# Turning q of two batches with TensorE transposes, weight sums on GpSimd, one halo copy a batch

## The chip, the cores and the metric

The kernel runs on one core of one Trainium2 chip. The metric is device time in microseconds (us) of one execution. All data are fp32; the engines are TensorE (PE), VectorE (DVE), ScalarE (ACT), GpSimd (POOL) and SyncE (SP, which here only issues DMAs).

## The reference

A linear attention without softmax, an RMS norm, and a gated linear unit whose gate is a causal convolution over five tokens:

```python
# q, k, v: (8 batches, 8 heads, 576 tokens, 64); w_val, w_out: (512, 512); conv_w: (5, 512)
kv  = einsum('bhsd,bhse->bhde', k, v)
o   = einsum('bhsd,bhde->bhse', q, kv)
x   = o / sqrt(mean(o * o, -1) + 1e-6) * g_norm        # heads side by side: (8, 576, 512)
gate_pre[t] = sum(conv_w[i] * x[t - 4 + i] for i in range(5))
out = (sigmoid(gate_pre) * (x @ w_val)) @ w_out
```

## The kernel before

The work is cut into small steps, each a Python function with a batch and a piece as arguments (`turn_q_rows 0 3` turns block 3 of batch 0). A long string `PLAN` (lines 19 to 204) lists the steps, and they are emitted in that order, so each engine's queue is the plan's order cut down to that engine's instructions. A tile framework adds the semaphore waits: an instruction waits for whoever wrote what it reads, read what it overwrites, or held its buffer before. PSUM is used as eight banks that are handed on from tile to tile.

**q.** The tokens of a batch are stored as 32 runs (t) of 18 (n), so that a token's neighbours lie 32 columns apart. For batches 0 and 1, `load_q_rows` puts q into the tile `qs` with the partition as (head, t) for four heads, once for each half r of the heads, and 18 rows n of 64 values in the free direction. `turn_q_rows b j` (line 471) turns a block j of four rows n (two in block 4) into a PSUM tile: for each n and r one matmul against the identity puts the 64 values of that half of the heads onto 64 partitions. `sort_q b j` (line 481) copies the tile to `qT`, 128 partitions at once, and sorts heads before tokens. Later batches are turned by DVE (`turn_q`).

**From q to the value product.** `kv_product` multiplies k and v, `kv_copy` (L450 for batch 0, L453 for others) takes the result out of PSUM, `raw_whole` (L512, batch 0) and `raw_pair` (L501) multiply qT with it; `square` (ACT), `sums` (DVE) and `powers` (POOL, L552) make the inverse root, `normalise` makes x, `turn_x` (PE, L583) and `keep_x` (ACT, L590) or, from batch 2 on, `turn_blocks` (DVE, L596) and `move_blocks` (DMA from SP and POOL, L604) make `xT`: channels on partitions, tokens in the free direction, with 128 columns ahead of them for the halo.

**The halo.** The first tokens of a run need the last four of the run before. `halo b` (line 608) fills the 128 columns in front from the last ones, shifted by one run, with one GpSimd copy (L611) for each of the four channel blocks kc. `gate_start` (ACT, L615), four `gate_tap` (DVE, L621) and `gate_end` (ACT, L628) make the gate.

**The weights.** They come as float64 and are narrowed on the chip in eight steps each (`narrow_weight`, L363 to L389 on DVE, L368 to L372 on ACT); this runs beside batches 0 and 1. The convolution weights (`cw`) come first: their steps on DVE and ACT end in `turn_cw` (PE, L414) and `keep_cw` (DVE, L418 to L420).

**The products.** Batches 0 and 1 use a plain value product (`val_product`, L633). From batch 2 on, and for the output product of all batches, the kernel uses a scheme with seven half-size products instead of eight (`val_fast`, L682, and `fast_product`, L774). It needs sums of blocks of the weights: `val_sums n` (line 649, into `vsum`) and `weight_sums n` (line 732, into `wsum`), four of each, 128 partitions x 512 elements, once for the whole kernel, on DVE. `x_sums` and `token_sums` make the sums of the other side.

Around the steps that matter most the plan reads (cut):

```
turn_q_rows 0 3; turn_q_rows 0 2; turn_q_rows 0 0; kv_product 0 0; turn_q_rows 0 1; sort_q 0 0; sort_q 0 1;
narrow_weight cw 0 3; narrow_weight cw 0 4; narrow_weight cw 0 7; turn_q_rows 0 4; turn_cw; keep_cw;
kv_product 0 1; sort_q 0 4; sort_q 0 3; kv_copy 0 0; kv_copy 0 1; ...; sort_q 0 2; raw_whole 0 3
...
move_blocks 2 0; move_blocks 2 2; move_blocks 2 1; ...; weight_sums 3; ...; kv_product 3 1; ...;
fast_product 0 0 6; move_blocks 2 3; raw_pair 3 3
```

Of the kernel before, what the change touches and what calls it, by code (L numbers as in the profile page):

```python
# [12 lines left out]
ALU = mybir.AluOpType  # L13
AX = mybir.AxisListType

P = 128
# [191 lines left out]
def kernel(  # L208
# [11 lines left out]
    nc = tc.nc  # L220
    B, H, S, D = q.shape
# [5 lines left out]
    NK = C // P  # L227
    TB = 32
    NB = S // TB
    K = moe_conv_w.shape[0]  # L230
    HALO = (K - 1) * TB
    SX = HALO + S
    HB = P // TB
# [19 lines left out]
    def ps(shape, name):  # L253
        return psum.tile(shape, FP32, tag="bank", bufs=8, name=name)
# [3 lines left out]
    ident = const.tile([P, P], FP32, name="ident")  # L258
    mhalf = const.tile([P, NJ * H + H // 2], FP32, name="mhalf")
    xTs = [const.tile([P, NK, SX], FP32, name=f"xT{i}") for i in range(2)]  # L260
# [9 lines left out]
    vsum = const.tile([P, 4, NK // 2, C // 2], FP32, name="vsum")  # L270
    wsum = const.tile([P, 4, NK // 2, C // 2], FP32, name="wsum")
    ys = [const.tile([P, C // TB, NJ, TB], FP32, name=f"y{i}") for i in range(2)]
    qs = const.tile([P, 3, NB, D], FP32, name="qs")
# [22 lines left out]
    st = {}  # L296
# [158 lines left out]
    def new_qT(b):  # L455
        if ("qT", b) not in st:
            st["qT", b] = work.tile([P, HP, S], FP32, tag="qT", name=f"qT{b}")
        return st["qT", b]
# [12 lines left out]
    def turn_q_rows(b, j):  # L471

        m = min(HB, NB - j * HB)
        pq = ps([P, HB, P], f"qTps{b}_{j}")
        for n in range(m):
            for r in range(2):
                nc.tensor.matmul(  # L477
                    pq[r * D:(r + 1) * D, n, :], qs[:, r, j * HB + n, :], ident[:], start=True, stop=True)
        st["pq", b, j] = pq

    def sort_q(b, j):

        m = min(HB, NB - j * HB)
        nc.scalar.copy(
            out=new_qT(b)[:].rearrange("p h (n t) -> p n h t", t=TB)[:, j * HB:j * HB + m],
            in_=st["pq", b, j][:, 0:m].rearrange("p n (h t) -> p n h t", t=TB))

    def raw_product(b, *chunks):

# [116 lines left out]
                in_=y[a * TB:(a + 1) * TB, i])  # L606

    def halo(b):
        for kc in range(NK):
            row = xTs[b % 2][:, kc, :].rearrange("p (n t) -> p n t", t=TB)  # L610
            nc.gpsimd.tensor_copy(row[:, 0:K - 1, 1:TB], row[:, NB:NB + K - 1, 0:TB - 1])  # L611

    def gate_start(b, jt):
        gate = work.tile([P, S], FP32, tag="gate", bufs=GATES, name=f"gate{b}_{jt}")
# [34 lines left out]
    def val_sums(n):  # L649

        one, two, op = (
            (wval[:, EVEN, HIGH], wval[:, ODD, HIGH], ALU.add),
            (vsum[:, 0], wval[:, EVEN, LOW], ALU.subtract),
            (wval[:, EVEN, LOW], wval[:, EVEN, HIGH], ALU.subtract),
            (wval[:, ODD, LOW], vsum[:, 1], ALU.subtract))[n]
        nc.vector.tensor_tensor(out=vsum[:, n], in0=one, in1=two, op=op)

    def x_sums(b, n):

# [72 lines left out]
    def weight_sums(n):  # L732
        one, two = (
            (wout[:, EVEN, HIGH], wout[:, EVEN, LOW]), (wout[:, ODD, HIGH], wsum[:, 0]),
            (wout[:, ODD, HIGH], wout[:, EVEN, HIGH]), (wout[:, ODD, LOW], wsum[:, 1]))[n]
        nc.vector.tensor_tensor(out=wsum[:, n], in0=one, in1=two, op=ALU.subtract)

    def token_sums(i, h, n):

# [62 lines left out]
    def store(i, c, queue=nc.sync, blocks=range(HB)):  # L802
# [5 lines left out]
    steps = {f.__name__: f for f in (  # L808
        load_half, load_q, load_q_rows, stage_weight, narrow_weight, turn_cw, keep_cw, start_warm, warm_up,
        kv_product, kv_copy, turn_q, turn_q_rows, sort_q, raw_whole, raw_pair, raw_tail, square, sums, powers, normalise,  # L810
        turn_x, keep_x, turn_blocks, move_blocks, halo, gate_start, gate_tap, gate_end, val_product, keep_val, gated,
        val_sums, x_sums, val_fast, val_keep, out_product, keep_out, weight_sums, token_sums, fast_product, fast_keep,
        store, store_last)}
    with tc.manual_schedule():
# [34 lines left out]
```

## Time and profile before

| | |
|---|---|
| timed runs | 305.83 and 306.24 us, median 306.03 |
| profiled execution, first to last instruction (span) | 304.6 us |
| the profiled execution's own time | not listed apart; the timed runs lie 1.2 to 1.6 us above the span |
| mean granted TensorE clock | 0.993 |
| PE busy | 294.8 us, 97% of the span |
| DVE busy | 269.2 us, 88% |
| ACT busy | 193.7 us, 64% |
| POOL busy | 114.9 us, 38% |
| PE on the turn (L477) | 144 records, 11.0 us |
| ACT on sort_q (L484) | 10 copies, 583 ns (512 columns) or 346 ns (256) each |
| DVE on the weight sums (L656, L736) | 8 instructions, 641 to 768 ns each |
| POOL on the halo (L611) | 32 copies, 17.5 us |

The profile is of one execution. A line of the groups names source line, engine, operation, tiles and shape, then busy time, mean duration and the idle time before. In the timeline a line gives start and duration in us, engine, line and operation; the square bracket says how long the engine had been idle and what released it. An fp32 matmul is two records, a transpose one. A queue's name with q (SPq) stands for the engine that issues a DMA. Matmul ends are modelled, so a busy PE can still be a PE that waits for little things.

### The profile page before, as it was taken

To read this page: it belongs to the slowest core of one execution; us is meant where nothing else is said; L and a number is where in the kernel's file an instruction comes from. 1 tells how busy PE (TensorE), PEld (TensorE's weight loads), DVE (VectorE), ACT (ScalarE), POOL (GpSimd) and SP (SyncE) were. 2 spreads that over 40 slices of the span, in tenths; PEclk is the share of its full clock that TensorE was granted. 3 is DMA by queue.
4 is the path that set the end of the run, shared out by engine and by line. 5 is a ranking of instruction groups with operands and counts; after the bars stand their busy time and mean duration, and the time that the engine had idled before them with its cause. 6 is when DMAs were issued, how large, how long until landed. Compare 5 with 4: busy or idle time off the path is not lost.

```text
span 304.6 us, 8977 instructions
## 1 busy us (share of the span) xinstructions
PE 294.8 (97%) x3441; PEld 232.4 (76%) x3441; DVE 269.2 (88%) x474; ACT 193.7 (64%) x596; POOL 114.9 (38%) x127
## 2 busy tenths in 40 slices
PE   7899999999999999999999999999999999999993
PEld 7788778877787785777778757787878588888582
DVE  1169999999999999999999999999999999999612
ACT  1569989999768664884586547683787354535220
POOL 3027354406568217364338352345536631000000
PEclk9979999999999999999999999999999999999999
DMA  7999998088569756988689477927411621112423
GB/s 269 343 368 343 272 302 210 4 230 269 154 147 329 231 163 167 269 220 260 173 253 294 111 175 232 326 72 214 114 48 30 169 80 34 36 42 64 103 69 103
DMA packets 32074, 55.53 MB, mean 182 GB/s; under 512 B 6166, under 2 KB 14358, under 8 KB 32032
## 3 DMA queue, kind: packets, MB, share of 16 engines
q1 hardware_dynamic: 29520, 49.76, 55.7%
q0 software_dynamic: 1632, 3.17, 4.1%
q10 hardware_dynamic: 880, 2.03, 1.8%
q8 instruction: 27, 0.44, 0.6%
q14 instruction: 15, 0.12, 0.1%
HBM read 39.21 MB, written 9.44 MB: 160 GB/s over the span
## 4 chain that ended last, share of the span: by engine, by line
PE 89%; DVE 5%; DMA 2%; issue 1%; ACT 1%; DVEq 0%; ACTq 0%; SPq 0%
PE a L774 18%; PE cb L774 14%; PE va L682 13%; PE val L633 11%; PE vc L682 6%; PE kvps L440 6%; PE raw L501 5%; PE out L720 5%; PE vb L682 4%; PE qTps L477 4%; PE raw L512 2%; PE xTps L583 2%; DMA qs<-in_q_dram 2%; DVE gate L621 2%; DVE xs L667 1%
## 5 line engine op out<-in xcount | busy, mean ns | idle before, releaser
L552 POOL TENSOR_TENSOR rt<-ss,mhalf 128x8 f32<-128x8 f32 (+3 forms) x38 | 68.9, 1822 | 101.0 <-DVE ss L544 100.8
L621 DVE SCALAR_TENSOR_TENSOR gate<-xT,cwT,gate 128x576 f32<-128x576 f32 x128 | 101.8, 809 | 1.0
L571 ACT ACTIVATE x<-raw,rt 128x64 f32<-128x64 f32 x252 | 55.8, 351 | 7.2 <-POOL rt L552 4.2
L604 POOL DMA_DIRECT2D xT<-y x48 | 26.4, 557 | 25.5 <-DVE ot L784 14.0
L633 PE MATMUL val<-xT,wval 128*128 128x288 f32 x128 | 33.0, 411 | 0.0
L774 PE MATMUL a<-wsum,sums 128*128 128x256 f32 x128 | 32.4, 382 | 0.0
L628 ACT ACTIVATE gate<-gate 128x576 f32<-128x576 f32 x32 | 22.0, 692 | 11.7 <-DVE gate L621 11.4
L633 PEld LDWEIGHTS val<-xT,wval 128*128 128x128 f32 x128 | 23.5, 190 | 6.5 <-ACT xT L590 0.4
L544 DVE TENSOR_REDUCE ss<-sq 128x8 f32<-128x520 f32 (+1 forms) x40 | 24.7, 627 | 2.9 <-ACT sq L531 2.5
L774 PEld LDWEIGHTS a<-wsum,sums 128*128 128x128 f32 x128 | 24.0, 190 | 4.1 <-issue 0.6
L535 ACT ACTIVATE sq<-raw 128x256 f32<-128x256 f32 (+1 forms) x70 | 22.4, 403 | 7.3 <-PE raw L501 7.1
L682 PE MATMUL va<-xs,vsum 128*128 128x288 f32 x96 | 26.6, 409 | 0.0
L615 ACT ACTIVATE gate<-xT,cwT 128x576 f32<-128x576 f32 x32 | 25.2, 811 | 1.5 <-DVE gv L646 1.3
L646 DVE TENSOR_TENSOR gv<-gv,gate 128x576 f32<-128x576 f32 x32 | 23.6, 750 | 0.9 <-ACT gate L628 0.8
L682 PEld LDWEIGHTS va<-xs,vsum 128*128 128x128 f32 x96 | 18.0, 190 | 5.1 <-ACT x L571 0.4
L611 POOL COPY xT<-xT 128x124 f32<-128x124 f32 x32 | 17.5, 585 | 10.5 <-ACT xT L590 10.5
L501 PEld LDWEIGHTS raw<-kv,qT 64*64 64x64 f32 x1008 | 16.4, 134 | 5.3 <-issue 3.0
L440 PEld LDWEIGHTS kvps<-v,k 64*64 64x64 f32 x1008 | 15.9, 135 | 3.7 <-issue 1.9
L501 PE MATMUL raw<-kv,qT 64*64 64x64 f32 x1008 | 18.7, 221 | 0.0
L440 PE MATMUL kvps<-v,k 64*64 64x64 f32 x1008 | 17.6, 220 | 0.0
L774 PE MATMUL cb<-wsum,sums 128*128 128x256 f32 x64 | 16.9, 386 | 0.1
L774 PE MATMUL cb<-wout,gv 128*128 128x256 f32 x64 | 16.8, 385 | 0.0
(111 smaller groups left out, 542.3 us busy)
## 6 DMA issues: line engine op xcount, KB each, us to landing
qs<-in_q_dram SPq DMA_DIRECT2D x96, 140.0 KB, 4.2
out_dram<-ot SPq DMA_DIRECT2D x140, 64.0 KB, 1.7
k<-in_k_dram SPq DMA_DIRECT2D x14, 576.0 KB, 6.3
v<-in_v_dram SPq DMA_DIRECT2D x12, 576.0 KB, 6.5
xT<-y SPq DMA_DIRECT2D x48, 64.0 KB, 2.7
xT<-y POOLq DMA_DIRECT2D x48, 64.0 KB, 3.3
y<-in_moe_w_val_dram SPq DMA_DIRECT2D x4, 512.0 KB, 11.4
w_wout<-in_moe_w_out_dram SPq DMA_DIRECT2D x4, 512.0 KB, 6.3
```

The lines of the kernel that those rows point to most:

```text
L440: nc.tensor.matmul(st["kvps", b][s][r * D:(r + 1) * D, i], st["k", b, i][rows, r, cols], st["v", b, i][rows, r, cols], start=(j == 0), sto ...
L501: nc.tensor.matmul(st["raw", b, c][r][cols, to * D:(to + 1) * D], st["qT", b][rows, hp, first:first + D], kvs[b % 2][rows, hp, :], start=T ...
L544: nc.vector.reduce_sum(out=st["ss", b][:, FIRST[c]:FIRST[c] + n], in_=st["sq", b, c][:, 0:n], axis=AX.X)
L552: nc.gpsimd.tensor_tensor(out=st["rt", b][:, which], in0=st["ss", b][:, which], in1=mhalf[:, which], op=ALU.pow)
L571: nc.scalar.activation(out=x[:, to * D:(to + 1) * D], in_=raw[:, h * D:(h + 1) * D], func=AF.Copy, scale=root[:, to:to + 1])
L604: (nc.sync if i % 2 else nc.gpsimd).dma_start(out=xTs[b % 2][i * TB:(i + 1) * TB, :, first:first + P], in_=y[a * TB:(a + 1) * TB, i])
L615: nc.scalar.activation(out=gate[:], in_=xTs[b % 2][:, jt, HALO:SX], func=AF.Copy, scale=cwT[:, K - 1, jt:jt + 1])
L621: nc.vector.scalar_tensor_tensor(out=gate[:], in0=xTs[b % 2][:, jt, tap * TB:tap * TB + S], scalar=cwT[:, tap, jt:jt + 1], in1=gate[:], op ...
L633: nc.tensor.matmul(val[:], wval[:, kc, jt * P:(jt + 1) * P], xTs[b % 2][:, kc, HALO + n * SV:HALO + (n + 1) * SV], start=(kc == 0), stop=( ...
L646: nc.vector.tensor_tensor(out=both, in0=both, in1=st["gate", b, jt][:], op=ALU.mult)
L682: nc.tensor.matmul(st[bank, "val", b, mj][:], weights_[:, k], tokens()[:, k], start=(n in (0, 1, 3) and k == 0), stop=(k == NK // 2 - 1), ...
L774: nc.tensor.matmul(st[bank, i, p], tokens()[:, k], weights_[:, k], start=(n < 2 and k == 0), stop=(k == NK // 2 - 1), skip_group_check=True)
```

## The change

Four edits; the plan stays as it is.

1. `turn_q_rows` transposes two rows n and n+1 at once (128 partitions x 128 values), so half e of the result's partitions holds the row of parity e. Half as many PE instructions are issued, each over the full width, and as transposes.
2. `sort_q` now makes four copies a block, one for each half r of the heads and parity e, from 64 partitions of PSUM to 64 of `qT`; where e is not r, they shift the data by 64 partitions. In batch 0 the two copies with e = 1 are on DVE, all others are on ACT.
3. `val_sums` and `weight_sums` run on GpSimd, at the same places in the plan.
4. `halo` is one GpSimd copy of all four channel blocks.

```diff
     def turn_q_rows(b, j):
         m = min(HB, NB - j * HB)
-        pq = ps([P, HB, P], f"qTps{b}_{j}")
-        for n in range(m):
-            for r in range(2):
-                nc.tensor.matmul(
-                    pq[r * D:(r + 1) * D, n, :], qs[:, r, j * HB + n, :], ident[:], start=True, stop=True)
+        pq = ps([P, 2, HB // 2, P], f"qTps{b}_{j}")
+        for r in range(2):
+            for n in range(0, m, 2):
+                nc.tensor.transpose(
+                    pq[:, r, n // 2, :], qs[:, r, j * HB + n:j * HB + n + 2, :].rearrange("p n d -> p (n d)"),
+                    ident[:])
         st["pq", b, j] = pq

     def sort_q(b, j):
         m = min(HB, NB - j * HB)
-        nc.scalar.copy(
-            out=new_qT(b)[:].rearrange("p h (n t) -> p n h t", t=TB)[:, j * HB:j * HB + m],
-            in_=st["pq", b, j][:, 0:m].rearrange("p n (h t) -> p n h t", t=TB))
+        for r in range(2):
+            for e in range(2):
+                (nc.vector.tensor_copy if b == 0 and e else nc.scalar.copy)(
+                    out=new_qT(b)[r * D:(r + 1) * D].rearrange("p h (n t) -> p n h t", t=TB)[
+                        :, j * HB + e:j * HB + m:2],
+                    in_=st["pq", b, j][e * D:(e + 1) * D, r, 0:m // 2].rearrange("p n (h t) -> p n h t", t=TB))
...
     def halo(b):
-        for kc in range(NK):
-            row = xTs[b % 2][:, kc, :].rearrange("p (n t) -> p n t", t=TB)
-            nc.gpsimd.tensor_copy(row[:, 0:K - 1, 1:TB], row[:, NB:NB + K - 1, 0:TB - 1])
+        rows = xTs[b % 2][:].rearrange("p k (n t) -> p k n t", t=TB)
+        nc.gpsimd.tensor_copy(rows[:, :, 0:K - 1, 1:TB], rows[:, :, NB:NB + K - 1, 0:TB - 1])
...
     def val_sums(n):
-        nc.vector.tensor_tensor(out=vsum[:, n], in0=one, in1=two, op=op)
+        nc.gpsimd.tensor_tensor(out=vsum[:, n], in0=one, in1=two, op=op)
...
     def weight_sums(n):
-        nc.vector.tensor_tensor(out=wsum[:, n], in0=one, in1=two, op=ALU.subtract)
+        nc.gpsimd.tensor_tensor(out=wsum[:, n], in0=one, in1=two, op=ALU.subtract)
```

## The prediction

> **What bounds the kernel now.** I read the busy shares, then the chain that ended last, then stretches of 5 us, then the timeline at the places the change touches.
>
> ```profile
> PE 294.8 (97%) x3441; PEld 232.4 (76%) x3441; DVE 269.2 (88%) x474; ACT 193.7 (64%) x596; POOL 114.9 (38%) x127
> ...
> PE 89%; DVE 5%; DMA 2%; issue 1%; ACT 1%; DVEq 0%; ACTq 0%; SPq 0%
> ```
>
> The chain lies on TensorE: time leaves the kernel only if PE work goes or PE's waits shrink, and a wait put on PE is not won back, since PE hardly idles later. But an average hides the stages:
>
> ```profile
> 15.00:20.00 5.00, 4.39 (x89) 3.82 (x89) 3.18 (x9) 3.38 (x9) 0.00 (x0) 0.73 0.95 341
> ...
> 25.00:30.00 5.00, 5.00 (x122) 4.32 (x122) 4.73 (x10) 4.57 (x9) 4.03 (x2) 1.00 0.86 321
> 30.00:35.00 5.00, 5.00 (x112) 4.06 (x104) 4.93 (x9) 4.68 (x11) 2.45 (x4) 1.00 0.95 293
> ...
> 45.00:50.00 5.00, 5.00 (x85) 3.93 (x84) 5.00 (x9) 5.00 (x21) 2.46 (x3) 1.00 1.05 254
> ```
>
> The columns after the stretch are its sum, then PE, PEld, DVE, ACT and POOL busy. From 25 to 80 us ACT is as full as PE (4.57, 4.68, 5.00 of 5), though its share of the span is 64%; the edited copies stand exactly there. DVE too is full from 30 us to 280 us.
>
> ```profile
> 6.12 5.05 PE L477 MATMUL qTps<-ident,qs 128*64 128x128 f32 x48 [0.70 <-DMA qs<-in_q_dram]
> ...
> 16.56 1.09 ACT L450 COPY kvbd<-kvps 64x128 f32<-64x128 f32 x4 [1.51 <-PE kvps L440]
> 17.15 6.32 PE L512 MATMUL raw<-kvbd,qT 128*128 128x128 f32 x40 [0.56 <-ACT kvbd L450]
> ...
> 23.40 2.84 PE L477 MATMUL qTps<-ident,qs 128*64 128x128 f32 x48
> ...
> 25.43 1.07 ACT L484 COPY qT<-qTps 128x512 f32<-128x512 f32 x2
> ...
> 29.97 2.04 ACT L590 ACTIVATE xT<-xTps 128x512 f32<-128x512 f32 x4
> ...
> 31.16 2.11 PE L633 MATMUL val<-xT,wval 128*128 128x288 f32 x8
> ```
>
> The releasers show who leads: kv_copy (L450) frees the raw products; keep_x (L590) frees the first val_product, 0.33 us after the copy it needs.
>
> **Part 1, the turn on PE.** Each block of four rows was 8 matmuls (16 records), now 4 transposes. The rows: 48 records in 2.77 us at 23.4 us (58 ns each, chain) against, for a transpose of 128x128:
>
> ```profile
> L583 PE MATMUL xTps<-ident,x 128*128 128x128 f32 x48 | 7.6, 281 | 0.0
> ```
>
> These start 109 ns apart. Batch 1 (18 rows): 4.23 us become 18 x 0.109 = 1.96, 2.3 us less. Batch 0 saves more, its first 48 records taking 5.05 us at half pace. Both are covered. Batch 0: the kv product that follows can start when k and v land (9.5 us instead of 11.1), but the second one stands behind turn_cw at 15.05, which waits for the conv-weight step on ACT (13.93); that one waits for no turn. Batch 1: what follows waits for ACT (next part). The earlier turns also free qs sooner for SP's loads of batch 1's q (issued at 13.88), and all behind them on SP; the DMA share is 0.94 and 0.95 of 10 to 20 us, so they land hardly earlier. I count nothing for PE; without the cover it would be 2.3 us, less in batch 0.
>
> **Part 2, the copies of batch 0.** One ACT copy a block (0.58 us) becomes four of 64 partitions, two on ACT, two on DVE. In the order of the built instructions each waits for the one before: ACT's second waits for DVE's first. Nearest rows: ACT 128x256 in 0.35 us (L484's short block), DVE 128x256 from PSUM in 0.42 (L797); of short blocks ACT 0.26 (L450), DVE about 0.29. Blocks 0 and 1 run 11.4 to 14.3 us, while ACT and DVE were idle, and leave L372 at about 13.9. Blocks 4 and 3 are caught: their DVE copies stand behind keep_cw, which ends at 15.92. From there 0.29 (DVE) + 0.26 (ACT) + 0.29 (DVE) + 0.42 (DVE) + 0.35 (ACT), with a little for the hand-overs, gives kv_copy at 17.5 instead of 16.56: +0.95. Block 2 then takes 0.35 + 0.42 + 0.35 instead of 0.58: +0.55. ACT is 1.5 us late; of that it gives back 0.99 in its wait for PE at 21.72. **+0.55** enters batch 1.
>
> The clock adds to it. The turns at 6.12 run at 105 ns a record, at 12.31 at 61; the clock rose at 10.5 after a stretch full of matmuls, and the 15 to 20 stretch, with gaps in it, was granted 0.73. After the change PE is idle from 8.7 to 9.5 and from about 12 to 15, so it may stay slow until 24 us: 24 raw records at 213 ns instead of 112 for part of the way, +0.9 on ACT's wait for the last raw product. Bounds 0 and 0.9; I take half, **+0.45**.
>
> The Trainium skill (TensorE: Matmul & The Clock Gate, Part 4) says that transposes do not count as activity for that gate. No row here shows it; by that rule the slow clock is sure, and the sum would be 0.45 higher.
>
> **Part 3, the copies of batch 1**, all four on ACT, in its full stretch. A 128x512 copy follows the next after 0.49 us (1.07 for two). Four of 256 columns cost between 4 x 0.25 (columns alone, 0.48 us per 512, and no fixed part less) and 4 x 0.35 (the short row in full); I take 0.28 each, 1.12, so +0.63 a block, +0.5 for the short one. Blocks 0, 2 and 3 precede keep_x: 1.9 less the 0.37 that ACT idled before 26.86: +1.5, with the entry 2.05 + 0.45. The first val_product (31.16) has 0.33 to spare: PE +1.7 + 0.45. Two more blocks stand before raw_pair 1 3 (ACT end 35.47, PE start 36.54: 1.07 to spare) and the third wval steps (38.30 on DVE, val_product at 39.96, together 0.97 to spare): ACT 3.1, PE **+2.1 + 0.45 = 2.55**. Bounds: +0.8 (0.25 a copy, DVE's part shorter) and +4.
>
> **Part 4, weight sums on GpSimd.** DVE loses eight instructions:
>
> ```profile
> L736 DVE TENSOR_TENSOR wsum<-wout,wsum x2: 651/666/682, 75.3 to 84.5; 128x512 f32<-128x512 f32 x2
> ```
>
> 8 x 0.68 = 5.4 us. GpSimd's price is not in the trace. Nearest is its copy of 124 elements:
>
> ```profile
> L611 POOL COPY xT<-xT x32: 276/690/906, 30.9 to 251.8; 128x124 f32<-128x124 f32 x32
> ...
> 82.66 4.44 POOL L604 DMA_DIRECT2D xT<-y  x8 [1.52 <-DVE ot L784]
> ...
> 85.94 1.13 PE L774 MATMUL a<-wsum,gv 128*128 128x256 f32 x4
> ```
>
> 0.28 free, 0.81 under a DVE instruction with two SBUF inputs. 512 elements: at least DVE's 0.67, at most 2 inputs x 4.13 x 0.28 = 2.3; I take one 4.13 x 0.28 = 1.15, plus 0.4 of waiting. (The Trainium skill, GPSIMD Engine Reference, Performance versus the Vector engine, gives 4.50 us for 2048 elements; a quarter is an estimate of 1.1, and the sum would be the same.)
>
> New wait: weight_sums 3 now stands on POOL behind six of the eight DMA issues of move_blocks 2. These end at 82.66 + 6 x 0.555 = 86.0; the sum ends at 87.2 to 87.6. DVE had it at 85.2 for the PE matmul at 85.94. PE waits **1.5 us** (bounds 0.7 and 2.5); behind it stand raw_pair 3 and all else. The last two DMA issues follow 1.5 us later, with 3 us to spare before x_sums. weight_sums 1 waits for a pow until 75.58 and ends near 77.0 for a matmul at 76.74: part of the same 1.5.
>
> DVE pays back: each sum makes its next two-input instruction wait. Halo copies stretched such a one from 0.75 to 0.83-0.86 for 124 elements; for 512 I take 0.7, bounds 0.3 and 1.2. 8 x 0.7 = 5.6 against 5.4: **0**, bounds -3 and +4.
>
> **Part 5, halo in one copy.** POOL issues one instead of four; DVE waits once for some 0.4 instead of up to four times for 0.02 to 0.11. **0**, bounds -0.5 and +1, covered by POOL's idle 62%; gate_tap waits longer for ACT's L615 than for it.
>
> **Sum.** 2.55 + 1.5 = +4.05. The span is 304.6; the two timed runs, 305.83 and 306.24, lie 1.4 above, so the profiled execution's own time is taken as 306.0, the median. 306.0 + 4.05 = **310.0**.
>
> **Rivals.**
> *DVE is what binds, and is relieved.* From 45 us on DVE is as full as PE. If a sum costs DVE under 0.3 us each (its next instruction often reads PSUM or one input), 3 us leave it; for this to count, PE's waits must come from DVE there, and weight_sums 3 must be in time. Then 306.0 + 2.55 - 5.4 = 303.2 at best. For: 5.00 of 5; against: PE fills the same stretches and the chain gives DVE 5%. It decides if PE's matmuls in 45 to 100 us move up by over 2.6 us.
> *Nothing net.* ACT's copies at 0.2 us and weight_sums 3 before 86: +0.5, 306.5. Against: ACT's 5.00, the six DMA issues.
> *DVE is blocked.* Each sum holds a DVE instruction for its whole 1.15 and the halos add 0.4: 8 x (1.15 - 0.68) + 1 = +4.5 on a full DVE, of which PE takes most: 310.0 + 3.5 = 313.5. For: 0.28 against 0.81; against: DVE has transposes and PSUM reads among its work. By the Trainium skill (SBUF - State Buffer, Who interferes with whom) the second to issue blocks for the whole instruction; the halo rows agree for 124 elements, none shows 512.
>
> **Chances.** Forecast 0.50 (308 to 312), blocked DVE 0.22, nothing net 0.16, relief 0.12. Two per cent of 306.0 is 6.1 us, about what a measurement of this kernel can tell from no change: below 299.9 or above 312.1. Faster 0.02 (the far end of relief), slower 0.24 (blocked and the edge of the forecast), within 0.74. The range leaves out a tenth on each side: 304.5 to 314.0; the forecast's own is 308 to 312.
>
> **What would show it.** Right: L450 near 17.5, first val_product at 33 or later, POOL's fourth wsum behind six DMA issues and PE waiting for it over 1 us, L484's successor in groups of 64 partitions near 0.3 us. Wrong: val_product at 31.5 or before, a GpSimd sum under 0.7 us, gate_tap unchanged at 810 ns beside the sums, or a PE that ends earlier though ACT is later.

## The result, and the profile after

The changed kernel took 315.09 us (314.57 to 315.60) against 306.03 before on the same chip: a ratio of 1.0306, with a 95% interval of 1.0245 to 1.0368. It is slower, as forecast, but by 9.1 us and not by 4.0; 310.0 and the range up to 314.0 were too low. Ratios below compare undisturbed runs alone, so they can differ by some tenths of a per cent from the ratio of two medians; the microseconds beside them are the ratio's excess times 304.4, the median of the kernel before on the later chips. There it ran 1.3 to 1.9 us faster than in its first two runs, and its only trace is of one of those; so these microseconds are mostly 1 to 2 us more than the lateness that a run's trace shows against that trace (e1, for one: 6.6 against 5.0).

First the head of the page of the changed kernel, answering the busy shares and the chain shown before, with the row of the granted clock (40 slices of 7.8 us):

```profile
PE 293.7 (94%) x3333; PEld 229.5 (73%) x3333; DVE 275.9 (88%) x476; ACT 199.4 (64%) x616; POOL 115.6 (37%) x111
...
PEclk9958699999999999999999999999999999999999
...
PE 76%; DVE 8%; ACT 6%; DMA 4%; issue 3%; POOL 1%; SPq 0%; ACTq 0%; DVEq 0%
```

PE has 108 records fewer and is busy 1.1 us less, but the span went from 304.6 to 313.8, so it idles 10.3 us more; ACT (1% of the chain before) and DVE (5%) hold more of it. DVE gave up 5.5 us of sums, was given ten copies of q, 4.0 us, and is busy 6.7 us more. The same stretches of 5 us as before:

```profile
15.00:20.00 5.00, 3.22 (x80) 2.98 (x81) 3.18 (x10) 2.61 (x9) 0.00 (x0) 0.61 1.05 406
...
25.00:30.00 5.00, 2.98 (x24) 2.29 (x22) 4.89 (x10) 4.91 (x12) 5.00 (x3) 0.98 0.40 160
30.00:35.00 5.00, 4.80 (x81) 3.96 (x82) 2.62 (x5) 4.83 (x11) 0.75 (x1) 0.50 0.85 239
```

From 25 to 30 us PE is busy 2.98 of 5 where it was full, and from 30 to 35 it is busy again, but at a granted clock of 0.50 where it had 0.95. The timeline of the same piece (start, length, engine, line; what ended the idle time before stands in brackets):

```profile
6.17 1.53 PE L477 MATMUL qTps<-ident,qs 128*128 128x128 f32 x12 [0.75 <-DMA qs<-in_q_dram]
...
17.82 1.09 ACT L450 COPY kvbd<-kvps 64x128 f32<-64x128 f32 x4
18.40 6.76 PE L516 MATMUL raw<-kvbd,qT 128*128 128x128 f32 x40 [1.71 <-ACT kvbd L450]
...
23.42 0.87 ACT L535 ACTIVATE sq<-raw 128x512 f32<-128x512 f32 x2 [0.67 <-PE raw L516]
...
25.56 1.06 ACT L535 ACTIVATE sq<-raw 128x512 f32<-128x512 f32 x2
27.13 3.02 ACT L487 COPY qT<-qTps 64x256 f32<-64x256 f32 x8
28.67 0.88 PE L477 MATMUL qTps<-ident,qs 128*128 128x128 f32 x6 [1.45 <-ACT qT L487]
30.20 1.74 PE L587 MATMUL xTps<-ident,x 128*128 128x128 f32 x6 [0.65 <-ACT qT L487]
31.87 2.53 PE L440 MATMUL kvps<-gv 64*64 64x64 f32 x72
34.33 1.97 PE L587 MATMUL xTps<-ident,x 128*128 128x128 f32 x8
36.09 2.36 PE L636 MATMUL val<-xT,wval 128*128 128x288 f32 x8
```

PE turns the first three blocks of batch 0 in 1.53 us (5.05 before). In batch 1 it waits for ACT's copies (1.45 and 0.65 us). Eight copies of batch 1 take 3.02 us, 0.378 each from start to start; before, one copy of 128 partitions stood in the place of four. The same 72 records of the kv product take 2.53 us (1.28 before), eight transposes of x 1.97 (1.09): half clock. The first val_product begins at 36.09 instead of 31.16.

Then the weight sums on GpSimd, with what they do to DVE, ACT and PE:

```profile
62.69 0.95 POOL L614 COPY xT<-xT 128x496 f32<-128x496 f32 x1
63.60 1.27 POOL L659 TENSOR_TENSOR vsum<-vsum,wval 128x512 f32<-128x512 f32 x1
63.86 1.56 DVE L389 SCALAR_TENSOR_TENSOR wout<-ot_wout,wexp_wout 128x512 f32<-128x512 f32 x1
65.51 1.78 POOL L739 TENSOR_TENSOR wsum<-wout 128x512 f32<-128x512 f32 x1 [0.63 <-DVE wout L389]
66.19 0.68 ACT L631 ACTIVATE gate<-gate 128x576 f32<-128x576 f32 x1 [0.79 <-DVE gate L624]
66.83 2.81 DVE L649 TENSOR_TENSOR gv<-gv,gate 128x576 f32<-128x576 f32 x2
67.25 1.78 POOL L659 TENSOR_TENSOR vsum<-wval 128x512 f32<-128x512 f32 x1
68.67 2.21 PE L636 MATMUL val<-xT,wval 128*128 128x288 f32 x8 [1.25 <-ACT xT L594]
...
90.12 3.36 POOL L608 DMA_DIRECT2D xT<-y  x6 [2.17 <-DVE ot L787]
93.50 1.28 POOL L739 TENSOR_TENSOR wsum<-wout,wsum 128x512 f32<-128x512 f32 x1
94.83 1.13 PE L777 MATMUL a<-wsum,gv 128*128 128x256 f32 x4 [1.17 <-POOL wsum L739]
```

A narrowing step of DVE (L389, 0.69 free) lasts 1.56 because val_sums 1 runs; the gate_tap behind it is late, so is the sigmoid on ACT (0.79 of idle time until DVE), so is keep_x behind that, and PE waits 1.25 us for it. The two gated products (L649) take 2.81 us instead of 1.38 under two sums, which are themselves stretched from 1.27 to 1.78. The fourth weight sum stands behind six DMA issues, and PE waits 1.17 us.

How late PE's same instructions start against the kernel before, read off the two traces:

| PE step (time before) | late by |
|---|---|
| turn_x 0 3 (26.17) | 0.43 |
| first val_product (31.16) | 4.93 |
| raw_pair 1 3 (36.54) | 5.45 |
| val_product 1 1 0 (61.62) | 7.05 |
| last matmuls of raw_pair 2 3 (65.62) | 7.68 |
| fast_product with weight_sums 3 (85.94) | 8.89 |
| end of the span | 9.2 |

So 5.0 us arise between 26 and 37 us, 1.25 at one val_product, 0.4 in a stop in the middle of a raw product (to which the last experiments come), 1.2 at weight_sums 3, and nothing after 95 us.

### The profile page after: what moved, and what is told of

Same layout as the page of the kernel before. It is cut to its first block, busy times and chain, and to the rows that moved or that the text cites. A ratio compares the mean times of both kernels' runs of the same rounds, so it can differ in the third digit from the quotient of the medians.

```text
span 313.8 us, 8762 instructions
## 1 busy us (share of the span) xinstructions
PE 293.7 (94%) x3333; PEld 229.5 (73%) x3333; DVE 275.9 (88%) x476; ACT 199.4 (64%) x616; POOL 115.6 (37%) x111
## 4 chain that ended last, share of the span: by engine, by line
PE 76%; DVE 8%; ACT 6%; DMA 4%; issue 3%; POOL 1%; SPq 0%; ACTq 0%; DVEq 0%
PE a L777 17%; PE va L685 15%; PE cb L777 14%; PE vc L685 7%; PE out L723 5%; PE raw L505 4%; PE kvps L440 4%; PE vb L685 4%; PE val L636 3%; DMA v<-in_v_dram 3%; DVE gate L624 2%; ACT qT L487 2%; PE xTps L587 2%; PE raw L516 2%; DMA out_dram<-ot 1%
## 5 line engine op out<-in xcount | busy, mean ns | idle before, releaser
L624 DVE SCALAR_TENSOR_TENSOR gate<-xT,cwT,gate 128x576 f32<-128x576 f32 x128 | 104.9, 833 | 1.5 <-ACT gate L618 0.4
L649 DVE TENSOR_TENSOR gv<-gv,gate 128x576 f32<-128x576 f32 x32 | 26.2, 832 | 1.0 <-ACT gate L631 0.9
L777 PE MATMUL a<-wsum,gv 128*128 128x256 f32 x64 | 16.7, 384 | 1.2 <-POOL wsum L739 1.2
L787 DVE TENSOR_TENSOR ot<-cb,ot 128x512 f32<-128x512 f32 x16 | 10.9, 682 | 7.1 <-DMA out_dram<-ot 4.1
## 6 DMA issues: line engine op xcount, KB each, us to landing
y<-in_moe_w_val_dram SPq DMA_DIRECT2D x4, 512.0 KB, 10.7
```

The costliest lines, as they stand in the source:

```text
L624: nc.vector.scalar_tensor_tensor(out=gate[:], in0=xTs[b % 2][:, jt, tap * TB:tap * TB + S], scalar=cwT[:, tap, jt:jt + 1], in1=gate[:], op ...
L649: nc.vector.tensor_tensor(out=both, in0=both, in1=st["gate", b, jt][:], op=ALU.mult)
L777: nc.tensor.matmul(st[bank, i, p], tokens()[:, k], weights_[:, k], start=(n < 2 and k == 0), stop=(k == NK // 2 - 1), skip_group_check=True)
```

## The experiments

### The three parts alone

e1_turn is the kernel before with turn_q_rows and sort_q of the change; e2_sums and e3_halo are these edits:

```
-        nc.vector.tensor_tensor(out=vsum[:, n], ...)      (and wsum)
+        nc.gpsimd.tensor_tensor(out=vsum[:, n], ...)
```
```
-        for kc in range(NK): ... nc.gpsimd.tensor_copy(one row)
+        nc.gpsimd.tensor_copy(rows[:, :, 0:K - 1, 1:TB], rows[:, :, NB:NB + K - 1, 0:TB - 1])
```

e1_turn: 

> Only the turn of q and its copies are changed; the sums stay on DVE, the halo in four copies. Theory 'the front': in the changed kernel PE was 5.45 us late at its raw product of 42 us, before any sum ran on GpSimd, and PE gives nothing back later: 306.0 + 5.4 = 311.4 us (310.5 to 312.3), eight ACT copies of batch 1 in about 3.0 us, a stretch of half clock near 30 to 37 us. Rival 'only as sized on record': +2.55, 308.6 us, the rest of the 9 us being the sums.

e2_sums: 

> Only the eight weight sums go to GpSimd. Theory 'port': a GpSimd sum of 1.27 us holds the DVE instruction with two SBUF inputs that comes after it, and the other way round (0.7 to 1.1 us each, 6.0 in all, against 5.4 us that leave DVE), and PE waits where such a DVE instruction has no slack: about 1.2 us before a val_product at 62 us, 0.6 soon after, 1.2 for weight_sums 3: +3 us, 309.0 (308 to 310). Rival 'queue only': DVE is even, only weight_sums 3 behind six DMA issues costs, +1.3: 307.3. Rival 'relief': 303 or below.

e3_halo: 

> Only the halo is one copy of 496 elements instead of four of 124. Theory 'even': DVE is held once for up to 1.1 us instead of four times for up to 0.1, POOL issues 24 instructions fewer: 306.0 within 0.6. Rival 'long lock': eight copies of 0.6 to 1.15 us each hold a DVE instruction for 0.2 to 0.4 us more, of which PE takes a part: +1 to +2 us. Rival 'gain': fewer hand-overs, -0.5 to -1 us.

Measured: e1 1.0218 (1.0185 to 1.0251), +6.6 us, the size of "the front"; e2 1.0064 (1.0035 to 1.0092), +1.9, less than "port" and nearer to "queue only"; e3 1.0014 (0.9991 to 1.0036), no difference that this measurement tells. Together 8.9 us. The changed kernel's 315.09 is 9.1 above the first two runs of the kernel before, but 10.7 above its later median of 304.4, so that the parts add up is shown only to within 2 us; the turn and its copies are the larger part either way. e1's stretch of half clock at 31.8 to 35.2 us is there as expected. In e2 a sum holds a DVE instruction as in the changed kernel, and "relief" is out.

Not all of e2's price lies with the sums, though. The first of them runs on GpSimd at 44.3 us, and before that PE stops in the middle of raw_pair 1 3:

```profile
34.00 0.56 PE L501 MATMUL raw<-kv,qT 64*64 64x64 f32 x21
35.60 1.14 PE L501 MATMUL raw<-kv,qT 64*64 64x64 f32 x59 [1.04 <-issue]
```

A packet of PE's instructions starts at 33.12 and takes 1.15 us, and PE goes on 1.33 us after its end; the last experiments come to such stops. Later PE waits 0.50 us at a val_product and 0.9 in all for two weight sums. How the 1.9 us divide between the stop and the sums no run settles.

### The turn taken apart

e4_onecopy keeps the new transposes and copies each block out in one piece, which leaves the rows of q in a wrong order; e5_copies keeps the old turn and copies in four; e7_actcopies takes DVE out of batch 0's copies:

```
e4  nc.scalar.copy(out=new_qT(b)...[:, j * HB:j * HB + m], in_=pq, all 128 partitions)   (cut)
e5  in_=st["pq", b, j][r * D:(r + 1) * D, e:m:2]           (same partitions, no shift)
e7  nc.scalar.copy(...) for all r, e in both batches
```

e4_onecopy: 

> The changed turn alone, but each block copied out in one ACT copy of 128 partitions, so that the halves are not shifted (the q rows stand in a wrong order; sums and halo as before). It shows what the transposes on PE do without the copies. Theory 'copies': ACT is as before, PE has 2.3 us less to do in batch 1: 305.0 to 306.0 us, and the first val_product at 31.2 us or a little before. Rival 'clock': the thinner work of PE is granted half clock until 24 us and again later, +1.5 to +2.2: 307.5 to 308.2.

e5_copies: 

> The old turn on PE (eight matmuls a block), but the copies out in the changed manner: four of 64 partitions a block, in batch 0 by ACT and DVE in turn, in batch 1 all by ACT. No half is shifted. Theory 'copies': the four copies cost what the turn alone cost beyond the transposes with one copy (311.73 - 307.71 = 4.0 us): before + 4.0 (3.4 to 4.6), with eight copies of batch 1 in about 3.0 us on ACT (0.378 each), and a clock as in the kernel before. Rival 'shift': part of the price is the shift between partitions, so copies without it are cheaper, near 0.25 each: before + 1.5 or less. Rival 'clock again': ACT's lateness thins PE out here too, with a second stretch of half clock: before + 5.5 or more.

e7_actcopies: 

> The changed turn alone (as e1), but in batch 0 too all four copies of a block on ACT, so that no copy waits for DVE. Theory 'hand-over': in e1 ACT stood idle 0.49 us at each of five DVE copies and the last ones stood behind DVE's conv-weight step; without them kv_copy begins 0.7 to 1.0 us earlier, and the time is 0.6 to 1.2 us below e1's. Rival 'ACT is full': four copies of 0.378 cost ACT as much as the hand-overs did: within 0.4 us of e1.

Measured: e4 1.0072 (1.0044 to 1.0101), +2.2 us; e5 1.0188 (1.0150 to 1.0227), +5.7; e7 1.0257 (1.0218 to 1.0296), +7.8. So the transposes cost by themselves, though they take work off PE: "copies" is out for e4, "clock" has the size. Its timeline shows the half clock in the same place as in the changed kernel:

```profile
28.98 0.89 PE L586 MATMUL xTps<-ident,x 128*128 128x128 f32 x6 [0.81 <-DVE x L564]
29.80 2.20 PE L440 MATMUL kvps<-gv 64*64 64x64 f32 x72
31.93 1.62 PE L586 MATMUL xTps<-ident,x 128*128 128x128 f32 x8
```

And the copies cost with the old turn too, more than "copies" gave them, and "shift" is out. The size is that of "clock again", but not for its reason: e5 has no second stretch of half clock. Its first one lasts 6.8 us where the kernel before had 3.4, and its eight copies of batch 1 are a little shorter than the shifted ones, 0.324 instead of 0.378:

```profile
27.74 2.59 ACT L486 COPY qT<-qTps 64x256 f32<-64x256 f32 x8 [0.21 <-PE qTps L477]
```

In e7 the hand-overs are gone and nothing is won: ACT's copies run on from 11.45 to 14.46 us, the conv-weight step L372 behind them starts at 14.46 instead of 13.91, turn_cw and the second kv product follow 0.5 to 0.6 us later, and kv_copy begins at 18.05 (17.82 in the changed kernel). "Hand-over" is out; e7 is 1.2 us above e1, where "ACT is full" gave at most 0.4, but the two intervals overlap.

### The clock

e6_twice issues every transpose of e4 twice to the same place, e6_matmul sends each of e4's pairs through an ordinary matmul (both with the rows of q in e4's wrong order), and e12_afterfill gives the whole changed kernel 32 small matmuls ahead of turn_cw and turn_x 0 3 four times over:

```
e6_twice   for _ in range(2): nc.tensor.transpose(pq[:, r, n // 2, :], ...)
e6_matmul  nc.tensor.matmul(pq[:, r, n // 2, :], pair, ident[:], start=True, stop=True)
e12        for _ in range(32): nc.tensor.matmul(bank[0:TB, D:D + TB], ident[:, 0:TB], ident[:, 0:TB], ...)
```

e6_twice: 

> As the kernel with the changed turn and one copy a block (e4), but every transpose is issued twice, to the same place, so that PE is as busy with the turn as before (8 x 0.109 = 0.87 us a block against 0.93); the q rows stand in a wrong order as in e4. Theory 'thin': what costs 2.2 us in e4 is that PE has too little to do for its clock; twice the transposes bring it back to before + 0.5 or less. Rival 'transposes do not count': the gate does not see transposes, so the second set does nothing for it: before + 2.2 or more. Under both the transposes themselves have room (PE waits there).

e6_matmul: 

> As e4 (pairs of rows turned, one ACT copy a block, q rows in a wrong order, sums and halo as before), but each pair goes through an ordinary matmul with the identity instead of a transpose: as many instructions as e4, and in the trace about two records of 0.11 us each, so PE is as busy with the turn as in the kernel before. Theory 'thin': e4's 2.2 to 3.2 us come from PE having too little work around the turns for its clock; here the time is before + 0.7 or less, and only one stretch of half clock is left. Rival 'the pairs themselves': something else of the new turn costs (the supply of instructions, the copies' reads): before + 2 or more, as e4 and e6_twice.

e12_afterfill: 

> The whole changed kernel, with PE kept busy at two places where it only waits: 32 small matmuls before turn_cw (12 to 15 us), and the four transposes of turn_x 0 3 issued four times (27 to 29 us). Theory 'clock': the second stretch of half clock (30 to 37 us) is gone and the first shorter; the first val_product begins near 34.5 us instead of 36.1 and the time is 1.5 to 2.5 us below the changed kernel's 1.03 x before. Rival 'ACT leads': ACT's copies end as late as before, PE waits for them instead of running slowly, and the gain is under 0.7 us.

Measured: e6_twice 1.0151 (1.0122 to 1.0180), e6_matmul 1.0112 (1.0064 to 1.0161), e12 1.0325 (1.0278 to 1.0373). By the times all three expectations of a gain fail. By the traces the clock did what "thin" says. The same kv product in e6_twice:

```profile
29.23 1.28 PE L440 MATMUL kvps<-gv 64*64 64x64 f32 x72
30.43 1.12 PE L587 MATMUL xTps<-ident,x 128*128 128x128 f32 x8
31.39 2.11 PE L637 MATMUL val<-xT,wval 128*128 128x288 f32 x8
```

Full clock; the first val_product stands at 31.39 (31.16 before, 33.39 in e4), in e6_matmul at 30.48. Part of what the two lose, they lose later: in each, PE stops for 1.3 us in all in two raw products (near 89 and 109 us), waiting for nothing that the profile names, 1.2 to 1.4 us after the end of a packet of its instructions; and e6_matmul waits 1.8 us for a late k near 142 us. By the traces e6_twice ends 3.1 us behind the kernel before and e6_matmul 2.5. So the times do not show what the full clock is worth.

In these traces the clock changes in steps of 3.41 us. Cut at these, here is the step ahead of the second half clock in the changed kernel (first line), and the same place in e6_twice (second line). PE runs nothing but transposes in both; its busy time is the third number, the granted clock the last but two:

```profile
26.36:29.77 3.41, 1.62 (x12) 1.06 (x10) 3.33 (x8) 3.33 (x9) 3.41 (x2) 1.00 0.17 67
25.72:29.14 3.42, 3.39 (x31) 3.10 (x29) 3.34 (x7) 3.17 (x7) 3.42 (x2) 1.00 0.44 162
29.14:32.55 3.41, 3.41 (x87) 3.00 (x86) 3.18 (x7) 3.33 (x7) 1.69 (x4) 1.00 0.64 174
```

The third line, e6_twice again, is what follows: full clock, where the changed kernel was granted 0.50. Over all kernels of this study the pattern has no exception: in the seven that turn batch 1 once by transposes (the changed kernel, e1, e4, e7, e12, e14, e18) a stretch of half clock begins between 26 and 34 us; in none of the other thirteen, the kernel before among them, does one begin after 18 us until PE's work ends. Until PE's work ends, a stretch lasts 3.41 us or a multiple of it. Where the limit lies is not shown, and the busy time does not decide alone: e4 has 1.89 of 3.41 us, transposes only, ahead of its half clock, while e13 and e16, described below, have 1.71 and 1.81 in the step of their stop near 39 us, other matmuls, and keep the full clock. So a transpose counts here, but whether as much as another matmul is open.

e12 tells less: its filler ran 61 of 64 records in 2.1 us and PE then stopped for 2.4, so that turn_cw came at 16.2 instead of 15.1 us; the second stretch shrank from 6.8 to 3.4 us, and the first val_product stood at 36.60. How much of the changed kernel's 9 us would come back with a full clock alone is not settled by it.

### The sums

e8_w3dve leaves weight_sums 3 on DVE; e9_late leaves val_sums 0, 1, 2 and weight_sums 0 on DVE; e10_nosums leaves the sums out and zeroes their tiles on GpSimd at the start:

```
e8   (nc.vector if n == 3 else nc.gpsimd).tensor_tensor(out=wsum[:, n], ...)
e9   (nc.gpsimd if n == 3 else nc.vector).tensor_tensor(out=vsum[:, n], ...)
     (nc.gpsimd if n else nc.vector).tensor_tensor(out=wsum[:, n], ...)
e10  nc.gpsimd.memset(vsum[:], 0.0); nc.gpsimd.memset(wsum[:], 0.0)
```

e8_w3dve: 

> Only the sums on GpSimd (as e2, before + 1.9 us), but weight_sums 3 stays on DVE. Theory 'queue': PE's wait of 0.7 us for weight_sums 3 behind six DMA issues, and the DVE instruction that it held for 1.87 us, are gone: before + 0.9 (0.5 to 1.3). Rival 'port alone': PE's loss comes from DVE instructions held by the other sums at 45 to 62 us: before + 1.7 to 1.9, as e2.

e9_late: 

> Only four of the eight sums go to GpSimd: weight_sums 1, 2, 3 and val_sums 3, all after 70 us; val_sums 0, 1, 2 and weight_sums 0 stay on DVE. Theory 'one place': the cost of the sums (e2: before + 1.9) is made at 60 to 70 us, where three sums and a halo copy follow each other on GpSimd and hold four DVE instructions; without these the time is before + 0.8 or less. Rival 'every sum costs', or the wait for weight_sums 3 is the larger part: before + 1.2 to 1.9.

e10_nosums: 

> The kernel before with all eight sums left out (zeros stand in their place, so the products that use them are wrong): DVE has 5.4 us less to do and nobody has more. It shows what DVE's relief alone is worth. Theory 'PE binds': before - 0.5 (-1.2 to +0.3). Rival 'DVE binds': before - 2 to -4, so that the port's holding gives away a real gain.

Measured: e8 1.0085 (1.0053 to 1.0117), +2.6 us, no better than e2, so "queue" is out; e9 1.0001 (0.9976 to 1.0027), no difference, within 0.8 us either way, as "one place" said. The waits of PE, first of e8, then of e9 (total, times, longest):

```profile
PE val L633 <- ACT xT L590: 1.4, 1, 1.4
```
```profile
PE a L774 <- POOL wsum L736: 0.9, 2, 0.5
```

e8 still has the wait near 61 us behind the three sums that follow a halo copy, and ends 1.4 us behind the trace of the kernel before. e9 has that no more and keeps the waits for GpSimd's weight sums: against the same trace its PE is 1.1 us late behind weight_sums 3 and 0.6 at the end. So in the traces the one place, from 60 to 70 us in the changed kernel, costs PE 1.25 us there, 1.4 in e8 and 0.5 in e2, and the waits for weight sums cost 1.2, 0.2 and 0.9; what each is worth in time by itself is too small for these ratios.

e10 went wrong as a time, 1.0149 (1.0102 to 1.0196): the zeroing on GpSimd stood ahead of the conv weight's load, and PE waited 5.6 us for turn_cw. Past that its trace can be read: PE is 3.9 us behind the kernel before at 25 us and 3.2 at the end, so taking 5.4 us off DVE gave back 0.7 by the traces. DVE's fullness does not bind.

### Each batch alone, and PE's instructions

e13_batch0 and e14_batch1 have the new turn and copies in one batch only. e15_cwfirst moves a step of the order of the kernel before:

```
-sort_q 0 0; sort_q 0 1; narrow_weight cw 0 3;
+narrow_weight cw 0 3; sort_q 0 0; sort_q 0 1;
```

e13_batch0: 

> The changed turn and copies for batch 0 alone; batch 1, the sums and the halo as before. On record this part stood at +0.55 plus 0.45 for the clock, 1.0 us, because ACT's delay was to be given back in its wait for PE at 21.7 us. Theory 'no slack': that wait is for the raw product, which starts later by as much as kv_copy (1.2 us), so nothing is given back, and the clock stays slow until 24 us: before + 2.5 (1.8 to 3.2). Rival 'as on record': before + 1.0 (0.5 to 1.5).

e14_batch1: 

> The changed turn and copies for batch 1 alone; batch 0, the sums and the halo as before. On record: three blocks at 4 x 0.28 instead of 0.49 on ACT, less 0.37 that ACT idled, and 0.33 that PE has to spare, then 2.1 us on PE. Theory 'pitch': a copy of 64 partitions takes its 0.378 us from start to start, so three blocks cost 2.9 more and five 4.3, less the same slacks: before + 3.3 (2.6 to 4.0). Rival 'as on record': before + 2.1 or less. Rival 'only together': the second stretch of half clock needs both batches, and without it batch 1 costs under 2.6.

e15_cwfirst: 

> Not the change: the kernel before with one step of the written order moved: narrow_weight cw 0 3 (ACT L372) stands ahead of sort_q 0 0 and 0 1 instead of behind them. In the traces this step ran at 12.3 to 12.6 us when the old turn had its full clock and at 13.9 when it had not, because it stood behind the copy of a block that PE turned late; turn_cw, the second kv product and the raw products follow it. Theory 'early': L372 at 11.5 us, turn_cw near 13.5 in every run, and 0.5 to 1.5 us less: before - 1.0. Rival 'something else is late next' (PE's supply of instructions while the DMA is full, the copies of q, the next weight): within 0.4 us of before.

Measured: e13 1.0274 (1.0251 to 1.0297), +8.3 us; e14 1.0319 (1.0303 to 1.0334), +9.7; e15 0.9998 (0.9979 to 1.0016). Each half alone costs more than both together (e1, 6.6), so no theory for e13 and e14 held; for e15 the rival that something else is late next did. e14's timeline shows why the halves cost so much:

```profile
38.50 1.38 PE L528 MATMUL raw<-kv,qT 64*64 64x64 f32 x75 [0.36 <-ACT kv L453]
42.34 0.38 PE L528 MATMUL raw<-kv,qT 64*64 64x64 f32 x5 [2.46 <-issue]
```

PE stops for 2.46 us after 75 of the 80 matmuls of one step. All operands of the step were there; "issue" means that the profile names no cause. The page has a row for the queue that brings PE's instructions, here of e14:

```profile
q8 instruction: 27, 0.44, 0.6%
```

27 packets for 0.44 MB are 16 KB each. In e14's trace one of them starts at 39.66, just as PE stops, and takes 1.13 us; PE goes on 1.55 us after its end. In e13 one starts at 38.67 in the same step, and PE stops from 39.4 to 41.2, until 1.27 us after its end. In the kernel before, packets started at 31.1 and 40.6 us and the step ran through between them. The new turn has 54 matmul records and 54 weight loads fewer in a batch, 108 instructions, and so moves where the blocks begin. Three kernels test that by the number of warm-up matmuls alone (9 in the kernel before; 63 in e13 and e14):

```
-start_warm 36;
+start_warm 9;        (e16; in e17 and e18: start_warm 63)
```

e16_shift: 

> Not the change: the kernel before with 9 instead of 36 warm-up matmuls at its start. By records that is 108 instructions less on PE, as many as the new turn takes away in one batch alone, so the 16 KB blocks in which PE's instructions arrive (the queue 'instruction' in the trace) begin elsewhere in the work. Theory 'supply': as in e13 and e14, PE stops in the middle of the raw product of 37 to 42 us for about 2 us, and again for 1 to 1.5 us near 108 us, while a block is under way: before + 3.5 (2.5 to 5). Rival 'nothing of the kind': the stops in e13 and e14 wait for something that the new turn itself makes late; here only the clock's rise comes later, before + 0 to 1.2.

e17_batch0pos: 

> e13 (the changed turn and copies for batch 0 alone) with 63 instead of 36 warm-up matmuls, so that the 108 instructions are there again and the blocks lie as in the kernel before. Theory 'supply': the stops at 39 and 111 us are gone, and what is left is the price of batch 0's copies: before + 2.0 (1.0 to 3.2), against e13's before + 7.9. Rival: e13's time stays, before + 6 or more.

e18_batch1pos: 

> e14 (the changed turn and copies for batch 1 alone) with 63 instead of 36 warm-up matmuls, so that the blocks lie as in the kernel before from batch 1 on. Theory 'supply': the stops of 2.7 and 1.2 us are gone: before + 5.0 (4.0 to 6.2), of which ACT's copies are about 3 and a second stretch of half clock (30 to 36 us) about 2. Rival: e14's time stays, before + 8.5 or more.

Measured: e16 1.0202 (1.0134 to 1.0270), +6.1 us; e17 1.0132 (1.0099 to 1.0164), +4.0; e18 1.0141 (1.0107 to 1.0174), +4.3. The stops are where "supply" puts them in all three, though its size was met in e18 alone (e16 cost more than the 5 us that it allowed, e17 more than 3.2): the kernel before, with 27 warm-up matmuls less, stops in the same step after the same 75 matmuls (first fence), and e13 with the instructions put back runs through (second fence):

```profile
36.97 1.38 PE L501 MATMUL raw<-kv,qT 64*64 64x64 f32 x75
39.94 0.33 PE L501 MATMUL raw<-kv,qT 64*64 64x64 f32 x5 [1.59 <-issue]
```
```profile
38.84 1.44 PE L528 MATMUL raw<-kv,qT 64*64 64x64 f32 x80
```

Of e16's 6.1 us its trace shows 4.1 against that of the kernel before: PE is 0.5 us late ahead of the first stop and 4.1 at the end, and three stops come to 3.2. e17 and e18 are the price of each batch with the blocks where they were: 4.0 and 4.3 us, against 6.6 for both. In e17's trace PE is 1.2 us late when the raw product starts and 2.2 when it ends, in a stretch of half clock from 14.0 to 24.2 us, and hardly later after that. In e18's PE goes from 2.1 us ahead at 24 us to 2.2 behind at 38.7. With both batches changed the stream has moved by 216 instructions, and the changed kernel stops only once, for 0.41 us at 73.3.

No kernel of these beats the kernel before; e9, e3 and e15 equal it. e15's earlier turn_cw (12.4 us, with the first val_product at 28.41 instead of 31.16) is not in the ratio: on the later chips the kernel before ran at medians of 304.2 to 304.7 us, 1.3 to 1.9 below its first two runs. Whether turn_cw came early there too, as the traces of e2, e3 and e4 show it with L372 at 12.5 us, is open; 56 of its 80 later runs were granted a mean clock of 0.995 or more, the traced one 0.993.

## Why the prediction was wrong, step by step

**The bound.** PE was the bound and stayed it: every wait put on it came out at the end. That ACT had no room from 25 us on, and that the loss would come there, was right.

**Part 1, the turn on PE, at 0.** This step failed. The 2.3 us of PE work were covered, as said, but the work that went was what kept the clock up between 25 and 30 us. (A reading in it was wrong as well: the conv-weight step on ACT, at 13.93, did stand behind a turn, since the copy ahead of it waited for one in the kernel before:

```profile
13.45 0.58 ACT L484 COPY qT<-qTps 128x512 f32<-128x512 f32 x1 [1.49 <-PE qTps L477]
```

With the four copies it came at 13.91 all the same.) The prediction let the clock stay slow until 24 us, 0.45 us with a bound of 0.9, and had no second stretch. Its price in the changed kernel by the same records: 2.53 - 1.28 for the kv product, 1.97 - 1.09 for eight transposes, 2.36 - 2.11 for the first val_product, 2.4 us in these three. (The six transposes of x at 30.20 took 1.74 instead of 0.87, but in part they wait for ACT.) e4 shows the transposes alone at +2.2, and e6_twice and e6_matmul show the stretch gone when PE is given as much to do.

The prediction set beside this a rule of the Trainium skill (TensorE: Matmul & The Clock Gate, Part 4), that transposes do not count as activity. Here the runs disagree: with every transpose issued twice, e6_twice kept full clock after 3.42 us of nothing but transposes (25.72 to 29.14, PE busy 3.39). Too little work is what the rows show; whether the kind of work matters as well, they leave open (e4 against e13 and e16, above).

**Part 2, batch 0, at 0.55 and 0.45.** kv_copy came at 17.82, against 17.5 forecast. The step that failed is "of that it gives back 0.99 in its wait for PE at 21.72". That wait was for the raw product, which waits for kv_copy and so came 1.25 us later itself; ACT still waited 0.67, gave back 0.3, and entered batch 1 1.7 us late (L535 at 25.56 instead of 23.86). A wait for something that the same change delays is no slack. The clock's 0.45 had the right sign: the first stretch of half clock lasted 6.8 us instead of 3.4, and the raw product, 1.25 late at its start, was 1.64 late at 22.82. e17 prices this batch at 4.0 us, and its trace at 2.2, where 1.0 stood.

**Part 3, batch 1, at 2.1.** The mechanism was right, the size was not: a copy took 0.378 instead of 0.28, twelve ahead of the val_product 4.5 us instead of 3.4 (1.65 before). PE's first val_product came at +4.9 and raw_pair 1 3 at +5.45 against +1.7 and +2.1, each with 0.45 for the clock. How the rest of this divides between ACT and the clock is only argued: without the slow clock PE would have waited for ACT for part of the time, as e5 does (0.86 us at its first val_product).

**Part 4, the sums.** The price on GpSimd, 1.15 plus 0.4, was near: 1.27 undisturbed, 1.6 to 1.8 when DVE was first. PE's wait for weight_sums 3, at 1.5, was 1.17. DVE's pay-back of 8 x 0.7 was near as a sum: the excess of the DVE instructions under the eight sums is 6.0 us, between 0 and 1.9 each. What failed is to set it against the 5.4 us saved and call the rest 0. DVE's average does not bind (e10), so the saving is worth little; held instructions in front of a chain that PE needs are paid: 1.25 us at 68.67, and 1.4 and 0.5 at the same step in e8 and e2. The 1.5 us stood at one sum where two places paid, and e9 bounds the four late sums, weight_sums 3 with them, at 0.8 us; in the changed kernel the lateness grew by 1.2 us at weight_sums 3 and stayed. Which of the two that wait is worth by itself is open.

The rival "DVE is blocked" had this mechanism, with the rule of the Trainium skill (SBUF — State Buffer, Who interferes with whom) that whoever issues first holds the shared ports for its whole instruction. The rows agree, for GpSimd as for DVE: 1.56 instead of 0.69 on L389, 1.78 instead of 1.27 on L659. Its price was taken over all sums (8 x 0.47 + 1 is 4.8, not 4.5); the time paid at two places. Its 313.5 came nearest to 315.1 by luck: it put the excess into the sums, and the runs put the larger part into the turn and its copies.

**Part 5, the halo, at 0.** Right: 1.0014.

**The sum.** On record 2.55 + 1.5 = 4.05. By the trace of the changed kernel 5.45 + 0.2 + 1.25 + 0.4 + 1.2 = 8.5 of the 8.9 that are there at 95 us. The largest miss is in the first term, 2.55 for what came to 5.45: the second half clock that stood at nothing in Part 1, the slack of Part 2 that was none, and copies at 0.28 that took 0.378. "Nothing net" and "relief" are out by e1 and e2.

## What to carry to other kernels

Work taken off the bounding engine is not free when that engine then waits for another one: in these traces the granted clock, too, fell where it was left with too little to do, so ask what fills the place. Idle time counts as slack only after you have asked whether what ends it is delayed by the same change; and a GpSimd instruction beside a full VectorE is priced by which VectorE instruction it holds, not by the average. Before reading small differences between variants, look whether PE stops in the middle of a step: 27 warm-up matmuls fewer moved this kernel by 6.1 us (4.1 to 8.2 by the interval).

## What the runs showed that was not expected

PE's supply of instructions is the largest. With 27 warm-up matmuls fewer and nothing else changed the kernel before lost 6.1 us, 3.2 of them in three stops of 0.6 to 1.6 us, each in a step of many 64x64 matmuls. These, the stops of e13 and e14 in the raw product of 37 to 42 us and the one of e2 each end 1.3 to 1.6 us after the end of a packet that brings a 16 KB block; e2 has as many instructions as the kernel before, so the number is not all that decides; what passes in that time no run explains. The Trainium skill (Runtime: NRT & Kernel Launch, Instruction fetch mechanics) has blocks of 16 KiB, which the row of the queue confirms, and calls the crossing of a boundary mostly hidden; in e13, e14 and e16 it was not.

One held instruction does not fit what Part 4 says of the shared ports: the gate_tap beside weight_sums 3 lasted 2.68 us (0.81 free) and began 0.77 us before the sum's own record, at the same place in the changed kernel, e2 and e9. Six DMA issues ran on GpSimd until the sum began; in the kernel before gate_taps ran beside the same issues in 0.82. This stays open.
